# A gated attention and feed-forward kernel on one core: the first attention tile's transposes move into the last gate/up unit, and the last down groups are spread between the output products

## The chip, the cores and the metric

The kernel runs on one core of one Trainium2 chip. The metric is the device time of one execution in microseconds (us), as the median of several executions; lower is better.

## The reference

The input `x` has 2048 rows of 576 values. A gate per row mixes two branches:

```python
g = sigmoid((x * gate_w).sum(-1, keepdims=True))
a = attention(x, wq, wk, wv, wo, beta)      # 32 heads of 18, 4 segments of 512 rows, with a memory carried on
b = (silu(x @ w_gate) * (x @ w_up)) @ w_down  # hidden width 4608
return g * a + (1 - g) * b
```

Inside the attention, each segment has softmax attention among its own 512 rows (`a_dot`) and a read of a memory of the earlier segments (`a_mem`); the two are mixed per head by `sigmoid(beta)`, and the result `o` is multiplied by `wo` (576 by 576). The four segments run one after another for the memory, which is empty for the first one.

## The kernel before

All matrix products are done in split form: a number is the sum of a high part (`hi`, made by ScalarE with a copy) and a low part (`lo`, made by VectorE as the source minus the high part), and a product becomes three matmuls, hi by hi, hi by lo and lo by hi.

The kernel first makes queries, keys, values and the memory reads and stores them in DRAM. The main part is a loop over 72 units: two halves of the rows (segments 2 and 3, then 0 and 1), and in each half 36 blocks of 128 hidden columns. In one unit, `seven(t, j)` issues seven blocks of seven matmuls, numbered j = 0 to 6, which give the gate and up products of that block for the half's 1024 rows (a seven-product scheme with sums of operands). ScalarE and VectorE turn the seven results into `silu(gate) * up`, in two row blocks, split into `hh` and `hl`. The order around a unit's end is: `seven(a, 4)`; ScalarE copies bank `a` to bank `xx` (line 1067); VectorE adds (1068); ScalarE loads the table for silu and does silu twice (1070, 1072), then loads the table for exp (989); `seven(y, 5)`; `seven(xx, 6)`, which adds to the bank that 1067 has filled; VectorE multiplies (1077, 1078); and the splits of the two row blocks to `hh` and `hl` follow (129 or 938 on ScalarE, 130 or 939 on VectorE). The banks a, xx and y are PSUM banks 0, 1 and 2.

Every third unit closes a group of three hidden blocks. The list `groups` then holds 16 down groups (8 row tiles by two column halves, of 320 and 256 columns). `down_group` issues nine matmuls for one of them (three hidden blocks by three split terms, line 856) into one PSUM bank and has VectorE add that bank to `ya` (line 861). In the middle of the kernel these groups are worked off in the next unit. The 16 groups of the very last unit have no next unit.

Work that must happen some steps later is put into `due` by `defer(k, fn)`; `beat()` takes out and runs one step's list. A unit has eight beats, k = 0 to 7, each after one of the `seven` blocks (two after block 5). Attention runs beside the units as a generator, one step per beat. When it has ended, `c_open` takes its memory over for the output stage: `wo` comes in six pieces of 96 columns (`wo_load`: a DMA, line 886; a high part on ScalarE, line 889; a low part on VectorE, line 890; three pieces for each column half of `wo`), and the first two attention tiles are loaded (`c_load`: `o`, line 895, and for rows with a memory `me`, line 899).

The output stage is the loop over n at the end, 16 tiles of 128 rows, written one tile ahead: step n prepares tile n and multiplies tile n - 1. `c_tr` prepares a tile: GpSimd adds `me` to `o` (911) and copies the last 64 columns (912), TensorE transposes five 128 by 128 blocks with the identity (915 to PSUM bank 5 or 6, 917 to bank 7), ScalarE and VectorE split the result into `oh` and `ol` (129, 130) and `os` (163, 164). `products` (line 152) multiplies a tile by one column half of `wo` in 14 matmuls into one of banks 0, 1, 2. VectorE then mixes with the feed-forward row tile `ff` (1127, 1128), and the rows are stored (1131, at the end 1133). `f_load` (906) fetches `ff` for the first half from DRAM. The down groups of the last unit are issued in the same loop, by `downs(k)`, and use banks 3 and 4 in turn.

The order on each engine is the order in which the Python code issues the instructions (`manual_schedule`); engines wait for one another through semaphores. All DMAs of this stage are issued from one queue, SP.

The tail that the change touches:

```python
ffs = {n: f_load(n) for n in range(2)}
for n in range(17):
    if n < 16:
        if n + 2 < 16:
            tiles[n + 2] = c_load(n + 2)
            ffs[n + 2] = f_load(n + 2)
        nxt = c_tr(*tiles.pop(n))
        downs(2 if n else 4)
    if n:
        ...
        for hf in range(2):
            t = chain_tile()
            products(t[:, :288], ops, w_mov(wos[hf], 288))
            downs(1)
            ...
    ops = nxt
```

Of the kernel before, what the change touches and what calls it, by code (L numbers as in the profile page):

```python
# [65 lines left out]
def gated_mix(ctx, tc, xT, xrest, wf, wfr, wfh, wd, wv, wo, beta, cmask, ident, bmask, out):  # L66
# [61 lines left out]
    def split(hi, lo, src):  # L128
        nc.scalar.activation(hi, src, AF.Copy)  # L129
        nc.vector.tensor_sub(lo, src, f32(hi))  # L130
# [31 lines left out]
    def xs_split(xs, raw):  # L162
        nc.scalar.activation(xs, raw, AF.Copy)
        nc.vector.tensor_sub(xs[64:128], raw[64:128], f32(xs[64:128]))
# [47 lines left out]
    def w_load(f, u):  # L212
        r = raw_tile().rearrange("p (k n) -> p k n", n=P)
        nc.sync.dma_start(r, wf[f][:, u, 0:4])
        return r
# [30 lines left out]
    def r_fetch(f):  # L246
        nc.sync.dma_start(f32(rhs[f % 2][:96]).rearrange("p j n -> p (j n)"), rc[f // 4, :, f % 4])
# [441 lines left out]
    with ExitStack() as st:  # L689
# [3 lines left out]
        def defer(k, fn):  # L693
            while len(due) < k:
                due.append([])
            due[k - 1].append(fn)
# [8 lines left out]
        def w_fetch(f):  # L705
            ops = wops[1, f] = [None] * 7

            def one(j):
                ops[j] = op_tile()
                nc.sync.dma_start(f32(ops[j]).rearrange("p a k n -> p (a k n)"), wc[f, j])  # L710

            return [(j + 2 if f else FIRST[j], lambda j=j: one(j)) for j in range(7)]
# [153 lines left out]
        wos, tiles = [], {}  # L866
# [42 lines left out]
        def c_tr(o, me):  # L909
            if me is not None:  # L910
                nc.gpsimd.tensor_add(o[:, 0:D], o[:, 0:D], me)
            nc.gpsimd.tensor_copy(o[:, 576:640], o[:, 512:576])
            ta = half_tile([P, 4, P])
            for k in range(4):
                nc.tensor.transpose(ta[:, k], o[:, P * k:P * k + P], idt)
            tb = lone_tile([P, P])
            nc.tensor.transpose(tb, o[:, 512:640], idt)
            oh = cps[0].tile([P, 4, P], F32R, name="oh")
            ol = cps[0].tile([P, 4, P], F32R, name="ol")
            os_ = cps[0].tile([P, P], F32R, name="os")  # L920
            split(oh, ol, ta)
            xs_split(os_, tb)
            r = []
            for k in range(4):
                r += [oh[:, k], ol[:, k], oh[:, k]]
            return r + [os_, os_]
# [30 lines left out]
        def feed(half, f):  # L957
            return [(f // CH, i, hf, hs, ds, yas[half], half) for i in range(8) for hf in range(2)]
# [32 lines left out]
        def seven(t, j, first=True):  # L991
# [6 lines left out]
                    n += 1  # L998
            nc.tensor.matmul(t, rem[:, RPOS[j]], XR[j], start=False, stop=True, skip_group_check=True)  # L999

        draw = {}
        for o, fn in start:
            defer(o - 7, fn)
        for pos, (half, f) in enumerate(seq):
            if f == 0:
                yas[half] = yp.tile([P, 8, D], F32, name="ya")
            q = f % CH
            nxt = seq[pos + 1] if pos + 1 < len(seq) else None
            if q == 0 and f:
                groups += feed(half, f - 1)  # L1010
            plan = []
            if nxt:
                plan += w_fetch(nxt[1]) if nxt[0] and nxt[1] < KEPT else w_make(*nxt)
                if nxt != (0, 1):
                    plan.append((1 if nxt[1] else 10, lambda f=nxt[1]: r_fetch(f)))
                for n, h in enumerate(BLOCKS.get(pos, ())):
                    plan += r_block(h, 4 * n)
                if f + 2 < FT:
                    wraw_of[f + 2] = [None, None]
                    for u in range(2):  # L1020
                        plan.append(((2, 5)[u] if f or not half else 5 + u, lambda u=u, f=f: wraw_of[f + 2].__setitem__(u, w_load(f + 2, u))))
            if pos == FT - 2:
                X2, XR2 = [[None, None] for _ in range(7)], [None] * 7
                plan += [(o + 8, fn) for o, fn in x_second(X2, XR2)]
            for o, fn in plan:
                defer(o + 1, fn)
            step = [0]

            def tick():
                k = step[0]  # L1030
                step[0] += 1
                if k == 0:
                    while stores:
                        nc.sync.dma_start(*stores.pop(0))
                if half == 0:
                    if (q, k) in ((0, 3), (1, 3), (2, 2)):
                        draw[f] = d_load(f)
                    if (q, k) in ((1, 1), (1, 7), (2, 4)):
                        g = f - 1 if k == 1 else f
                        ds[half, g] = d_split(g, draw.pop(g))  # L1040
                elif (q, k) in ((1, 0), (1, 2), (2, 1)):
                    g = f - 1 if k == 0 else f
                    ds[half, g] = d_fetch(g)
                beat(k, half)

            ops, rem = wops.pop((half, f)), rhs[f % 2]
            hh = fp.tile([P, 2, L], F32R, name="hh")
            hl = fp.tile([P, 2, L], F32R, name="hl")
            hs[half, f] = hh, hl
            a, y, xx = a_tile(), y_tile(), x_tile()  # L1050
            p5, sg0, sg1 = (row_tile() for _ in range(3))
            seven(a, 0)
            nc.scalar.activation(xx, a, AF.Copy)  # L1053
            tick()
            seven(y, 1)
            nc.scalar.activation(p5, y, AF.Copy)
            tick()
            seven(a, 2, False)
            y = y_tile()
            nc.vector.tensor_add(y, a, p5)  # L1060
            tick()
            seven(xx, 3, False)
            nc.scalar.activation(sg0, xx, AF.Copy)  # L1063
            tick()
            seven(a, 4, False)
            xx = x_tile()
            nc.scalar.activation(xx, a, AF.Copy)  # L1067
            nc.vector.tensor_add(p5, a, p5)  # L1068
            tick()
            nc.scalar.activation(sg0, sg0, AF.Silu)  # L1070
            seven(y, 5, False)
            nc.scalar.activation(sg1, y, AF.Silu)
            exp_table()
            tick()
            tick()
            seven(xx, 6, False)
            nc.vector.tensor_mul(sg0, xx, sg0)
            nc.vector.tensor_mul(sg1, p5, sg1)
            if q == CH - 1:
                defer(2, lambda t=(hh[:, 0], hl[:, 0], sg0): split(*t))  # L1080
            else:
                split_by(2, hh[:, 0], hl[:, 0], sg0)
            split_by(3, hh[:, 1], hl[:, 1], sg1)
            tick()
            assert not groups
            if f == FT - 1:
                groups += feed(half, f)
                if half == 0:
                    for n in range(BREAK):
                        beat(None if n > 1 else n)  # L1090
                    XO, XR = X2, XR2
                    assert not groups
# [13 lines left out]
        def downs(k):  # L1106
            for _ in range(min(k, len(groups))):
                down_group(*groups.pop(0))
# [4 lines that stand above are left out]
                if n + 2 < 16:  # L1113
                    tiles[n + 2] = c_load(n + 2)
                    ffs[n + 2] = f_load(n + 2)
                nxt = c_tr(*tiles.pop(n))
                downs(2 if n else 4)
            if n:
                tt = order[n - 1]
                ff = ffs.pop(n - 1)  # L1120
                for hf in range(2):
                    c = slice(288 * hf, 288 * hf + 288)
# [3 lines that stand above are left out]
                    if hf == 0:  # L1126
                        nc.vector.tensor_scalar_mul(ff, ff, g1[:, tt:tt + 1])
                    nc.vector.scalar_tensor_tensor(ff[:, c], t[:, :288], gg[:, tt:tt + 1], ff[:, c],
                                                   op0=OP.mult, op1=OP.add)
                    if hf == 0 and sent:  # L1130
                        nc.sync.dma_start(*sent.pop(0))
                    if n == 16:
                        nc.sync.dma_start(out[0, P * tt:P * tt + P, c], ff[:, c])
                if n < 16:
                    sent.append((out[0, P * tt:P * tt + P, :], ff))
            ops = nxt
# [54 lines left out]
```

## Time and profile before

| what | value |
|---|---|
| median of 3 runs | 1755.48 us (1752.46 to 1756.5) |
| the profiled execution's own time | 1755.81 us |
| its span, first to last instruction | 1754.1 us |
| granted TensorE clock, mean | 0.995 |
| TensorE (PE) busy | 1718.9 us, 98% |
| VectorE (DVE) busy | 1373.2 us, 78% |
| ScalarE (ACT) busy | 1094.7 us, 62% |
| GpSimd (POOL) busy | 935.5 us, 53% |

The execution's own time is 1.7 us longer than the span; what lies outside the span is launch and end. In a timeline row, the columns are the start (us from the span's start), the length, the engine, the line, the operation, what it writes and reads, the count, and in brackets the time that the engine stood idle just before and what released it. PEld is TensorE's loading of weights, which runs beside its matmuls. Matmuls overlap, so the pace of TensorE is the distance between starts and not the length of one.

### The profile page before, as it was taken

The page shows a single profiled execution, that of the slowest core. Times are in us where ns is not written, and L with a number is a line of the kernel's source. Part 1 is how long each engine was busy: PE and PEld are TensorE (multiplying, and loading weights), DVE is VectorE, ACT ScalarE, POOL GpSimd, SP SyncE. Part 2 cuts the span into 40 slices and gives each one's busy share as a digit, 9 for nine tenths or more (in the row PEclk, how much of TensorE's full clock was granted, in tenths as well). Part 3 has the DMA queues.
Part 4 walks back from the last instruction along what each step waited for, and adds up shares of the span by engine and source line. Part 5 has one row for each costly group of instructions (what it writes and reads, how often), then busy time and mean ns, then how long its engine had stood idle before and what let it go on. Part 6 is the DMA issues. An engine that isn't in the chain of part 4 may idle for free.

```text
span 1754.1 us, 34945 instructions
## 1 busy us (share of the span) xinstructions
PE 1718.9 (98%) x11868; PEld 1487.7 (85%) x11868; DVE 1373.2 (78%) x3239; ACT 1094.7 (62%) x2201; POOL 935.5 (53%) x1194
## 2 busy tenths in 40 slices
PE   9999999999999999999999999999999999999999
PEld 7898878888888878887887888888888888888799
DVE  6567577988898888898889777788788777887655
ACT  7665575765776577576666756665765576556511
POOL 4434546566665656665566455555555555555221
PEclk9999999999999999999999999999999999999999
DMA  8653589999998988998889976876787667866544
GB/s 288 220 188 113 168 285 188 214 203 191 231 217 189 199 193 194 178 219 189 192 175 248 282 170 141 187 169 160 160 179 170 148 165 179 169 127 156 167 132 140
DMA packets 524003, 328.06 MB, mean 187 GB/s; under 512 B 411184, under 2 KB 460336, under 8 KB 523824
## 3 DMA queue, kind: packets, MB, share of 16 engines
q1 hardware_dynamic: 523824, 325.83, 76.6%
q8 instruction: 93, 1.52, 0.4%
q14 instruction: 86, 0.70, 0.1%
HBM read 165.76 MB, written 76.09 MB: 138 GB/s over the span
## 4 chain that ended last, share of the span: by engine, by line
PE 77%; ACT 9%; DVE 5%; issue 3%; DMA 3%; POOL 2%; SPq 1%; DVEq 0%; ACTq 0%; POOLq 0%
PE bank L996 29%; PE bank L856 24%; PE bank L152 10%; PE bank L999 5%; PE bank L725 3%; PE bank L773 2%; ACT L1070 1%; PE bank L774 1%; DMA pt<-p 1%; ACT L989 1%; ACT pe L743 1%; PE bank L411 1%; DVE hl L939 1%; PE bank L457 1%; DMA draw<-in_wd_dram 1%
## 5 line engine op out<-in xcount | busy, mean ns | idle before, releaser
L758 POOL TENSOR_TENSOR p<-pe,p 128x512 f16<-128x512 f32 x320 | 374.3, 1170 | 459.2 <-DVE p L757 440.4
L856 PE MATMUL bank<-dw,hh 128*128 128x320 f32 (+1 forms) x2304 | 490.4, 306 | 4.3 <-ACT hh L129 2.1
L856 PEld LDWEIGHTS bank<-dw,hh 128*128 128x128 f32 x2304 | 382.8, 190 | 15.7 <-DVE ya L861 2.6
L743 ACT ACTIVATE pe<-bank,mb 128x512 f32<-128x512 f32 (+3 forms) x512 | 246.1, 522 | 219.9 <-DVE mb L731 217.0
L856 PE MATMUL bank<-dw,hl 128*128 128x320 f32 (+1 forms) x1152 | 341.2, 296 | 0.2 <-DVE hl L130 0.2
L731 DVE CUSTOM_DVE_ANT_0 scr<-bank,cm 128x512 bf16<-128x512 f32 (+3 forms) x512 | 246.1, 481 | 7.4 <-PE bank L725 0.6
L856 PEld LDWEIGHTS bank<-dw,hl 128*128 128x128 f32 x1152 | 218.7, 190 | 0.4 <-DVE hl L130 0.4
L861 DVE TENSOR_TENSOR ya<-bank,ya 128x320 f32<-128x320 f32 x352 | 157.5, 452 | 78.2 <-PE bank L856 77.3
L999 PE MATMUL bank<-xr,rh 128*128 128x512 f32 x504 | 197.0, 391 | 0.0
L751 POOL TENSOR_SCALAR_AFFINE_SELECT pe<-pe 128x256 f32<-128x256 f32 (+1 forms) x320 | 150.8, 472 | 31.2 <-ACT pe L743 25.0
L757 DVE CAST p<-pe 128x512 f16<-128x512 f32 x320 | 145.2, 454 | 2.9 <-DMA pt<-p 2.7
L257 POOL TENSOR_TENSOR ws<-raw 128x256 f32<-128x256 f32 x140 | 122.9, 878 | 19.6 <-DMA raw<-in_wf_dram 6.4
L725 PE MATMUL bank<-kst,qst 108*128 108x512 bf16 (+3 forms) x512 | 125.4, 306 | 5.2 <-ACT pe L743 5.1
L999 PEld LDWEIGHTS bank<-xr,rh 128*128 128x128 f32 x504 | 95.0, 188 | 20.5
L939 DVE TENSOR_TENSOR hl<-row,hh 128x512 fp32r<-128x512 f32 x120 | 100.9, 841 | 10.4 <-ACT hh L938 10.0
L1063 ACT ACTIVATE row<-bank 128x512 f32<-128x512 f32 x72 | 43.1, 598 | 96.2 <-PE bank L999 96.1
L1068 DVE TENSOR_TENSOR row<-bank,row 128x512 f32<-128x512 f32 x72 | 49.6, 689 | 56.5 <-ACT bank L1067 56.3
L1070 ACT ACT_TABLE_LOAD x72 | 92.4, 1283 | 1.3
L989 ACT ACT_TABLE_LOAD x72 | 92.4, 1283 | 1.0
L773 PE MATMUL bank<-v,pt 128*128 128x57 bf16 x1280 | 77.3, 188 | 8.5 <-DMA pt<-p 5.3
L1053 ACT ACTIVATE bank<-bank 128x512 f32<-128x512 f32 x72 | 41.7, 579 | 66.7 <-PE bank L999 66.7
L773 PEld LDWEIGHTS <-pt 128*128 128x128 f16 x1280 | 69.6, 96 | 16.1 <-issue 7.2
(2165 smaller groups left out, 4127.2 us busy)
## 6 DMA issues: line engine op xcount, KB each, us to landing
raw<-in_wf_dram SPq DMA_DIRECT2D x140, 256.0 KB
rh<-rc SPq DMA_DIRECT2D x72, 336.0 KB
dc<-dw SPq DMA_DIRECT2D x36, 576.0 KB
dw<-dc SPq DMA_DIRECT2D x36, 576.0 KB
stk<-q SPq DMA_DIRECT2D x32, 384.0 KB
draw<-in_wd_dram SPq DMA_DIRECT2D x36, 288.0 KB
rc<-rt SPq DMA_DIRECT2D x42, 224.0 KB
vd<-vps SPq DMA_DIRECT2D x8, 912.0 KB
```

Source lines behind the costliest of these rows:

```text
L152: nc.tensor.matmul(t, st[n], mv[n], start=(n == 0), stop=(n == 13))
L725: nc.tensor.matmul(t[:, c:c + w], qs[:KR, pr, P * i:P * i + P], ks[:KR, pr, 0:w], start=True, stop=True)
L731: nc.vector.tensor_tensor_reduce(scr[:, :w], t[:, c:c + w], cm[:, L - w:L], -SCALE, 3.0e38, OP.add, OP.min, m[:, k:k + 1])
L743: nc.scalar.activation(pe[:, c:c + w], t[:, c:c + w], AF.Exp, bias=m[:, k:k + 1], scale=SCALE)
L751: nc.gpsimd.affine_select(d, d, pattern=pat, compare_op=OP.is_ge, fill=0.0, base=0, channel_multiplier=1)
L757: nc.vector.tensor_copy(p[:, 0], pe)
L758: nc.gpsimd.tensor_sub(p[:, 1], pe, p[:, 0])
L773: nc.tensor.matmul(t[:, pr, i, :], pt[:, c], v, start=(n == 0), stop=False, skip_group_check=True)
L856: nc.tensor.matmul(t, p, q[:, cs], start=(n == 0), stop=(n == 3 * CH - 1))
L861: nc.vector.tensor_add(ya[:, i, cs], t, ya[:, i, cs])
L996: nc.tensor.matmul(t, w[:, p, z], x[z][:, q], start=first and n == 0, stop=False, skip_group_check=True)
L999: nc.tensor.matmul(t, rem[:, RPOS[j]], XR[j], start=False, stop=True, skip_group_check=True)
```

## The change

The last unit (the only one without a next unit) gets one more planned step: three steps on in its plan, which is at its beat k = 3, right after `seven(xx, 3)`, `c_tr` of tile 0 is issued. The loop at the end then takes the result from the list `early` at n = 0. The numbers of down groups per step change as well: none at n = 0 and none ahead of the products at n = 1. Before, the 16 groups lay 4, 4, 4, 4 on n = 0, 1, 2, 3; now they lie 2, 4, 4, 4, 2 on n = 1 to 5. No instruction is added or removed.

```diff
+        early = []
         draw = {}
         ...
             plan = []
+            if not nxt:
+                plan.append((3, lambda: early.append(c_tr(*tiles.pop(0)))))
             if nxt:
         ...
                     tiles[n + 2] = c_load(n + 2)
                     ffs[n + 2] = f_load(n + 2)
-                nxt = c_tr(*tiles.pop(n))
-                downs(2 if n else 4)
+                nxt = c_tr(*tiles.pop(n)) if n else early.pop()
+                downs(2 if n > 1 else 0)
```

The order of TensorE's work from the last unit's block 3 on, where tr(n) is the five transposes of tile n, P(n, h) the 14 products of tile n with column half h, and g0, g1, ... the down groups:

```text
before: seven 3, seven 4, seven 5, seven 6, tr0, g0, g1, g2, g3, tr1, g4, g5, P(0,0), g6, P(0,1), g7, tr2, ...
after:  seven 3, tr0, seven 4, seven 5, seven 6, tr1, P(0,0), g0, P(0,1), g1, tr2, g2, g3, P(1,0), g4, P(1,1), g5, tr3, ...
```

On ScalarE the two splits of tile 0 (129, 163) now stand behind the fourth `wo` piece (889) and ahead of the copy 1067 of the last unit. On VectorE the two splits of tile 0 (130, 164) now stand ahead of 1068, with the `wo` pieces three and four (890), 1077 and 1078 behind them. GpSimd's order and SP's order of DMAs are the same as before.

## The prediction

> **What bounds the kernel now.** I read the page's engine shares first, then busy time by stretches around the last unit, then the waits of TensorE in that stretch, then each engine's timeline there.
>
> ```profile
> span 1754.1 us, 34945 instructions
> PE 1718.9 (98%) x11868; PEld 1487.7 (85%) x11868; DVE 1373.2 (78%) x3239; ACT 1094.7 (62%) x2201; POOL 935.5 (53%) x1194
> ```
>
> The stretches after the last unit (length, then busy time of PE, PEld, DVE, ACT, POOL, granted clock, DMA share, GB/s):
>
> ```profile
> 1659.00:1662.50 3.50, 1.38 (x11) 1.11 (x9) 2.94 (x6) 3.47 (x7) 0.55 (x1) 1.00 1.10 360
> 1662.50:1668.00 5.50, 4.18 (x27) 3.72 (x28) 4.07 (x8) 1.13 (x3) 3.51 (x4) 1.00 0.62 231
> 1668.00:1695.50 27.50, 27.50 (x212) 27.50 (x211) 12.28 (x26) 2.30 (x6) 5.57 (x6) 1.00 0.37 119
> ```
>
> The waits of TensorE from 1653 to 1669:
>
> ```profile
> PE bank L856 <- ACT hh L129: 2.1, 1, 2.1
> PE bank L856 <- DVE ya L861: 1.1, 1, 1.1
> ```
>
> TensorE is busy 98% of the span, so an edit can only win where it stands still or by taking work off it, and this one takes none off. The stretches show where it stands still: 1.38 of 3.50 us busy right after the last unit, 4.18 of 5.50 us next, and then 27.50 of 27.50. The waits name what ends it: the first down group waits for the high part `hh` of the last hidden block, and the third for VectorE to empty its bank. TensorE's timeline gives the places.
>
> ```profile
> 1653.58 1.52 PE L996 MATMUL bank<-xo,wo__22970 128*128 128x512 f32 x6
> 1655.17 1.52 PE L996 MATMUL bank<-xo,wo__22994 128*128 128x512 f32 x6
> 1657.07 1.65 PE L996 MATMUL bank<-xo,wo__23009 128*128 128x512 f32 x6 [0.15 <-ACT bank L1067]
> 1658.79 0.60 PE L915 MATMUL bank<-idt,o 128*128 128x128 f32 x4
> 1659.26 0.54 PE L856 MATMUL bank<-dw,hh 128*128 128x320 f32 x2
> ...
> 1662.52 0.56 PE L856 MATMUL bank<-dw,hh 128*128 128x320 f32 x2 [2.14 <-ACT hh L129]
> 1663.49 0.40 PE L856 MATMUL bank<-dw,hh 128*128 128x256 f32 x2
> 1665.86 0.56 PE L856 MATMUL bank<-dw,hh 128*128 128x320 f32 x2 [1.14 <-DVE ya L861]
> 1668.83 0.54 PE L856 MATMUL bank<-dw,hh 128*128 128x320 f32 x2
> ```
>
> The chain of waits further on:
>
> ```profile
> 1671.47 1.86 PE bank L152 x14
> 1673.33 1.32 PE bank L856 x9
> ...
> 1676.51 1.08 PE bank L856 x9
> ```
>
> In the timeline, the first three rows start blocks 4, 5 and 6 of the last unit; block 5 follows block 4 by 1.59 us, so block 6 could start at 1656.76 and starts at 1657.07: 0.31 us late. Then tr0 at 1658.79 (0.47 us to the next start), g0 at 1659.26, g1 at 1663.49, g2 at 1665.86, and after g3 and tr1 comes g4 at 1668.83. The rows of the chain give the pace without waits: a product half 1.86 us, a down group 1.32 us (320 columns) or 1.08 us (256).
>
> From 1658.79 to 1668.83 are 10.04 us. The work in it is tr0 0.47, four groups 2 x 1.32 + 2 x 1.08 = 4.80, and tr1 0.47: 5.74 us. So 4.30 us are lost here, and the 0.31 us before block 6. That is all that the change can win: at most 4.6 us, 0.26% of the time. What a measurement of this kernel can tell from no change is about 0.2%, 3.5 us.
>
> **The change, part by part.** I follow each engine through the changed order. The timelines of ScalarE, VectorE and GpSimd have the rows that set the times:
>
> ```profile
> 1655.93 0.61 ACT L889 ACTIVATE wo<-raw 128x480 fp32r<-128x480 f32 x1 [0.98 <-DMA raw<-in_wo_dram]
> 1656.44 0.58 ACT L1067 ACTIVATE bank<-bank 128x512 f32<-128x512 f32 x1
> 1660.87 1.08 ACT L889 ACTIVATE wo<-raw 128x480 fp32r<-128x480 f32 x2
> 1661.85 0.61 ACT L129 ACTIVATE hh<-row 128x512 fp32r<-128x512 f32 x1
> 1662.89 0.57 ACT L129 ACTIVATE oh<-bank 128x512 fp32r<-128x512 f32 x1
> 1663.37 0.26 ACT L163 ACTIVATE os<-bank 128x128 fp32r<-128x128 f32 x1
> ...
> 1657.05 0.69 DVE L1068 TENSOR_TENSOR row<-bank,row 128x512 f32<-128x512 f32 x1 [2.27 <-ACT bank L1067]
> 1657.66 2.42 DVE L890 TENSOR_TENSOR wo<-raw,wo 128x480 fp32r<-128x480 f32 x2
> 1662.50 0.69 DVE L130 TENSOR_TENSOR hl<-row,hh 128x512 fp32r<-128x512 f32 x1 [0.35 <-ACT hh L129]
> 1663.11 0.65 DVE L890 TENSOR_TENSOR wo<-raw,wo 128x480 fp32r<-128x480 f32 x1
> 1663.67 0.68 DVE L939 TENSOR_TENSOR hl<-row,hh 128x512 fp32r<-128x512 f32 x1
> 1664.28 0.68 DVE L130 TENSOR_TENSOR ol<-bank,oh 128x512 fp32r<-128x512 f32 x1
> 1664.99 0.29 DVE L164 TENSOR_TENSOR os<-bank,os 64x128 fp32r<-64x128 f32 x1
> ...
> 1650.34 0.31 POOL L912 COPY o<-o 128x64 f32<-128x64 f32 x1
> 1657.51 1.44 POOL L911 TENSOR_TENSOR o<-o,me 128x576 f32<-128x576 f32 x1 [6.86 <-DMA me<-med]
> 1659.01 0.55 POOL L912 COPY o<-o 128x64 f32<-128x64 f32 x1
> 1664.01 1.62 POOL L911 TENSOR_TENSOR o<-o,me 128x576 f32<-128x576 f32 x1 [4.44 <-DMA me<-med]
> ```
>
> Transposes moved (tr0). GpSimd has tile 0 ready at 1650.65 (the 912 row), TensorE comes to it after block 3 at 1653.58: no wait, 0.47 us. Blocks 4 and 5 start at 1654.05 and 1655.64, and block 6 could start at 1657.23.
>
> ScalarE's two splits moved. They are queued behind the fourth `wo` piece (889), which waited for its DMA until 1655.93, and the copy 1067, on which block 6 waits, is now queued behind them. By the rows' starts, 889 to the next is 0.51 us, the `oh` split to the next 0.48, and the `os` split 0.26: `oh` starts at 1656.44, `os` at 1656.92, 1067 at 1657.18 instead of 1656.44. So 0.74 us go on the path: block 6 starts at 1657.81 instead of 1657.07 and ends its pace at 1659.53. All that ScalarE does after 1067 follows back to back up to `hh` (table, two silus, table, two `wo` pieces), so `hh` is 0.74 us later too: it starts at 1662.59, and the row of 1662.52 for TensorE becomes 1663.26. The next two steps hide part of it.
>
> tr1 and products. tr1 needs GpSimd's tile 1, done at 1659.56 (1659.01 + 0.55), so it runs to 1660.03. P(0,0) runs to 1661.89. Its low parts: VectorE's order is now `ol` and `os` of tile 0 (0.61 + 0.3 us, from 1657.05), 1068 to 1658.6, and then the `wo` pieces three and four; GpSimd's add ends at 1658.95, so piece three is done at 1659.6, before the third matmul of P(0,0) at 1660.3. No wait.
>
> g0. Two of its three blocks run from 1661.89 to 1662.77, then it waits for `hh` at 1663.26. Before, g0 ended at 1663.49, with `hh` and the wait for `hl` in it; the same 0.74 us later is 1664.23. So the wait of 2.1 us shrinks to 0.5.
>
> P(0,1). It needs the last `wo` piece's low part, 0.74 us later than 1663.76: 1664.50. Its third matmul comes at 1664.49. It just fits, and it ends at 1666.09; g1 to 1667.17. tr2 needs GpSimd's tile 2: the add is ready to start at 1664.01 and lasts 1.44 us, and after the copy the tile is there by about 1666.4. No wait; tr2 to 1667.64.
>
> g2's bank. VectorE must have emptied g0's bank, behind the second `hl` (939), `ol` and `os` of tile 1. I estimate from the rows that 939 is held up by GpSimd's add until 1665.93, as the two 890 were at 1657.66 (2.42 us for two that take 0.65 each, with an add of 1.44 us beside them). Then 0.6 for 939, 1.0 for the splits, 0.5 for the bank: 1668.0. So g2 waits 0.36 us instead of the 1.14 before.
>
> Sum. The changed kernel starts g2 at 1668.0 with tr0, tr1, tr2, P(0,0), P(0,1), g0 and g1 done. The kernel before starts g4 at 1668.83 with tr0, tr1 and g0 to g3 done. The changed one is ahead by tr2 0.47 and two halves 3.72, less g2 and g3 2.40: 1.79 us of work. The gain is 1668.83 - 1668.0 + 1.79 = 2.6 us.
>
> After that. Two groups move from n = 0 to n = 4 and 5, where TensorE has no gaps to fill, at 1.32 + 1.08 us, already in the sum. The tail is bound by TensorE (27.50 of 27.50 us). SP's order and GpSimd's are unchanged; the tile loads wait for the buffers of transposed tiles, which come free earlier. I put later effects at nothing; what would uncover them is a load landing after its tile's turn.
>
> The profiled execution took 1755.81 us; less 2.6 is 1753.2. The median of the runs is 0.33 us lower, so it goes to 1752.9. I forecast 1753.0.
>
> [...] The 890 row is VectorE work with both inputs in SBUF, which took 2.42 us instead of 1.3 while GpSimd added. In the row of 1664.01 it is the other way round: GpSimd's add took 1.62 us, where 939 had started before it. [...]
>
> **The rivals.**
>
> First, the early landing: ScalarE's fourth piece does not hold up the copy, since its DMA lands 0.7 us or more earlier. Then `hh` is ready at 1662.5 as before, g0 ends at 1663.3, P(0,1) waits 0.2 us for the last low part and ends at 1665.4, g2 starts at 1666.9 with its bank free: 1668.83 - 1666.9 + 1.79 = 3.7 us, 1752.1. For it: landing times hang on a queue at a DMA share of 1.10 and vary. Against it: in this trace the piece ended a ScalarE wait of 0.98 us.
>
> Second, the lost lock: the last `wo` piece's low part on VectorE should start at 1663.85, GpSimd's add at 1664.01. If the add is first by 0.2 us, the piece waits to 1665.45 and is ready at 1666.1; P(0,1) stands from 1664.49 to 1666.1, ends at 1667.7, and g2 starts at 1669.25: 1.4 us gained, 1754.4. For it: only 0.16 us decide. Against it: nothing else on VectorE is queued ahead.
>
> Third, slower: the `wo` pieces become the wait. Before, P(0,0) came at about 1671.3 and the last low part at 1663.76, 7.5 us of slack; now P(0,1) needs it at 1664.49 and has none. Each microsecond that the last two pieces land late is then one of TensorE, past the point where ScalarE is free for them (1660.87). From 2.6 us late on the kernel is slower than before; 6.1 us late costs 0.2%, at 1759.3. For it: the DMA engines are full in that stretch. Against it: 889 ran the two at 1660.87 without a wait for a DMA, and SP's order is unchanged.
>
> That the change does not do what it says is excluded by the order of instructions: the five transposes do stand after block 3.
>
> **How the numbers follow.** Forecast 0.42, early landing 0.30, lost lock 0.18, late pieces 0.10. The three runs before lie 4 us apart, so a median of a few can be off by 1.5 us. The forecast's 2.6 us then read as over 3.5 about one time in three (0.15), the early landing's 3.7 six in ten (0.18), the lost lock's seldom (0.03): faster 0.36. Slower by over 0.2% needs the late pieces (0.08). The rest, 0.56, is within 0.2%. The range reaches from the early landing less 1.9 us (1750.2) to the lost lock with 1.6 us of scatter (1756.0).
>
> **What would show it.** Right: tr0 in the unit at no wait; 1067 about 0.7 us later; `products` ahead of g0; the wait for `hh` at about 0.5 us instead of 2.1; no wait above 0.5 us for `ya`; and the rest of the tail without a gap. Wrong: a wait of TensorE at the transposes (tile 0 late), at P(0,1) for the last `wo` piece of over 1 us, or at later transposes for GpSimd; or a time beyond the range with this stretch as forecast, which would put the cause elsewhere.

## The result: 4.8 us faster

| | kernel before | changed kernel |
|---|---|---|
| median of 22 runs | 1755.44 us | 1750.65 us |
| lowest to highest | 1749.49 to 1761.92 us | 1746.59 to 1753.4 us |
| profiled execution, its span | 1755.81 us, 1754.1 us | 1749.81 us, 1748.1 us |

The ratio is 0.9974 with a 95% interval of 0.9967 to 0.9982: between 3.2 and 5.8 us faster. The page of the changed kernel has the same shares as before:

```profile
span 1748.1 us, 34944 instructions
PE 1716.3 (98%) x11868; PEld 1484.9 (85%) x11868; DVE 1372.0 (78%) x3239; ACT 1094.5 (63%) x2201; POOL 935.1 (53%) x1194
```

TensorE's timeline after the last unit's block 3:

```profile
1650.89 0.60 PE L915 MATMUL bank<-idt,o 128*128 128x128 f32 x4
...
1651.35 1.64 PE L996 MATMUL bank<-xo,wo__22970 128*128 128x512 f32 x6
...
1654.72 1.65 PE L996 MATMUL bank<-xo,wo__23009 128*128 128x512 f32 x6
...
1656.44 0.60 PE L915 MATMUL bank<-idt,o 128*128 128x128 f32 x4
...
1656.91 0.38 PE L152 MATMUL bank<-wo,oh 128*128 128x288 f32 x1
...
1658.84 0.46 PE L856 MATMUL bank<-dw,hh 128*128 128x320 f32 x2
...
1660.17 0.55 PE L856 MATMUL bank<-dw,hh 128*128 128x320 f32 x2 [0.29 <-ACT hh L129]
1660.89 0.41 PE L856 MATMUL bank<-dw,hl 128*128 128x320 f32 x1 [0.17 <-DVE hl L130]
1661.15 0.30 PE L152 MATMUL bank<-wo,oh 128*128 128x288 f32 x1
...
1663.15 0.40 PE L856 MATMUL bank<-dw,hh 128*128 128x256 f32 x2
...
1664.24 0.60 PE L915 MATMUL bank<-idt,o 128*128 128x128 f32 x4
...
1664.70 0.54 PE L856 MATMUL bank<-dw,hh 128*128 128x320 f32 x2
```

The rows are, in order: tr0, blocks 4 and 6, tr1, the start of P(0,0), g0, its two short waits, P(0,1), g1, tr2, and g2. The waits of 2.14 us for `hh` and 1.14 us for g0's bank have become 0.29 us and nothing.

To compare kernels that reach this place a few us apart, I use one length from here on. The **tail** is the time from the start of TensorE's next work after block 3 to the end of the span. It was 1754.1 - 1653.58 = 100.5 us before and is 1748.1 - 1650.89 = 97.2 us now: 3.3 us less. The other 2.7 us between the two spans lie ahead of anything the change touches.

### The profile page after: what moved, and what is told of

It reads as the page before. It is cut to its first block, busy times and chain, and to the rows that moved or that the text cites. A ratio compares the mean times of both kernels' runs of the same rounds, so it can differ in the third digit from the quotient of the medians.

```text
span 1748.1 us, 34944 instructions
## 1 busy us (share of the span) xinstructions
PE 1716.3 (98%) x11868; PEld 1484.9 (85%) x11868; DVE 1372.0 (78%) x3239; ACT 1094.5 (63%) x2201; POOL 935.1 (53%) x1194
## 4 chain that ended last, share of the span: by engine, by line
PE 76%; ACT 9%; DVE 5%; issue 4%; DMA 3%; POOL 3%; SPq 0%; DVEq 0%; ACTq 0%; POOLq 0%
PE bank L996 29%; PE bank L856 23%; PE bank L152 9%; PE bank L999 5%; PE bank L725 3%; PE bank L773 2%; ACT L1073 1%; DMA pt<-p 1%; PE bank L774 1%; ACT L989 1%; PE bank L411 1%; ACT pe L743 1%; DVE scr L731 1%; PE bank L457 1%; POOL ws L257 1%
## 5 line engine op out<-in xcount | busy, mean ns | idle before, releaser
L939 DVE TENSOR_TENSOR hl<-row,hh 128x512 fp32r<-128x512 f32 x120 | 101.7, 847 | 10.7 <-ACT hh L938 10.3
L152 PE MATMUL bank<-xo,qhi 128*128 128x512 f32 x264 | 83.1, 396 | 0.0
```

Source lines behind the costliest of these rows:

```text
L152: nc.tensor.matmul(t, st[n], mv[n], start=(n == 0), stop=(n == 13))
```

## The experiments

**The same two programs again.** Is the part ahead of the tail shorter too, or is that scatter?

> The changed kernel once more, beside a second run of the kernel before. I call tail the time from the end of block 3's matmuls in the last unit to the end of the span: 100.5 us in the profile before, 97.2 us in the profile after, so 3.3 us of the 6.0 us between the two spans. Theory A (the gain is TensorE's standstill after the last unit, filled with products): the tail is 97.2 us again, within 0.5, and the rest of the difference between two spans lies ahead of it and changes its sign or size. Theory B (the change also shortens what lies ahead of the last unit, for example through where memory lies): the tail differs by 3.3 us and the part ahead is shorter by 1 to 3 us again.

> The kernel before, unchanged. Theory A: the tail is 100.5 us within 0.7 us (its waits hang on when the fourth wo piece lands), and the part ahead of it scatters by a few us from run to run. Theory B: the part ahead is again 1 to 3 us longer than that of the changed kernel in the same call.

The changed kernel came to 1750.39 us (ratio 0.9975, 0.9965 to 0.9985), with a tail of 1747.7 - 1650.40 = 97.3 us. The kernel before came to 1756.11 us against its own other runs on that chip (ratio 1.0012, 1.0002 to 1.0021, for the same program, so a difference of some 0.1% is not to be trusted in such a comparison). Its block 3 ended at 1649.98 us, earlier than in the changed kernel (1650.89, 1650.40): theory B falls, the part ahead only scatters. The granted clock, the share of full speed at which the profile shows TensorE running, goes with that scatter. Ahead of block 3's end TensorE's clock stood at half for some 10 us in this profile and in both of the changed kernel, and for some 17 us in the first profile before. Over all thirteen profiles of this document, with tr0 taken off where it stands ahead, block 3 ends at 1649.9 to 1650.9 us where that time was 10 us (once at 1652.5), at 1651.7 to 1652.8 where it was 14, and at 1653.6 where it was 17. But the tail of the second profile before was 1752.6 - 1649.98 = 102.6 us, 2.1 us more than in the first profile, and outside theory A's 0.7 us. TensorE's timeline there:

```profile
1658.62 0.56 PE L856 MATMUL bank<-dw,hh 128*128 128x320 f32 x2 [2.12 <-ACT hh L129]
...
1661.96 0.90 PE L856 MATMUL bank<-dw,hh 128*128 128x320 f32 x2 [0.94 <-DVE ya L861]
...
1662.93 0.74 PE L856 MATMUL bank<-dw,hh 128*128 128x320 f32 x2
```

The waits are as before, yet the matmuls after them are slow: a pair of 320 columns is 0.74 us long instead of 0.46. The busy time by stretches of this run has the reason (columns as before: length, busy time of PE, PEld, DVE, ACT and POOL, granted clock, DMA share, GB/s):

```profile
1655.00:1660.00 5.00, 2.71 (x19) 2.19 (x18) 4.44 (x8) 4.70 (x10) 0.61 (x2) 1.00 1.10 363
1660.00:1665.00 5.00, 4.06 (x19) 3.77 (x19) 2.41 (x6) 0.00 (x0) 3.56 (x4) 0.55 0.40 149
1665.00:1670.00 5.00, 5.00 (x33) 5.00 (x33) 2.17 (x5) 0.77 (x2) 0.00 (x0) 0.77 0.27 75
```

The granted clock, third column from the end, is 0.55 and 0.77. In finer stretches it fell to 0.50 at about 1660.5, 2 us after the standstill, and came back at about 1667.3 us. In the first profile before it was 1.00 throughout this stretch, and in the changed kernel's profile too:

```profile
1660.00:1665.00 5.00, 4.66 (x33) 4.28 (x34) 4.75 (x10) 1.35 (x5) 3.35 (x3) 1.00 1.05 390
1665.00:1670.00 5.00, 5.00 (x39) 5.00 (x38) 2.19 (x5) 0.70 (x2) 2.11 (x4) 1.00 0.69 233
```

**One half of the change: transposes early, groups as before.**

```diff
-                downs(2 if n > 1 else 0)
+                downs(2 if n else 4)
```

> Half of the change: tile 0 is transposed in the last unit, but the down groups stay at 4, 4, 4, 4 on n = 0 to 3. Theory A (products must fill the wait for hh): the wait of g0 for hh stays at 2 us or more, since the transposes no longer stand ahead of it; only the wait for g0's bank shrinks, by up to 1.1 us, since tile 0's two VectorE splits have gone from the queue ahead of it. The tail is 99.5 to 100.5 us. Rival (the moved transposes are the gain): the tail is 97 to 98 us.

1755.03 us, ratio 1.0001 (0.9992 to 1.0010). TensorE's only wait in the stretch:

```profile
PE bank L856 <- ACT hh L129: 2.7, 1, 2.7
```

The wait for `hh` grew, the wait for the bank is gone, both as theory A has it. The tail is 1753.5 - 1651.69 = 101.8 us: above the forecast of 99.5 to 100.5, with a clock that fell here too (0.53 from 1660 to 1665), and 0.8 us below the kernel before with a fallen clock. The moved transposes alone are not the gain.

**The other half: groups spread, transposes as before** (`downs(2 if n > 1 else 0)` in the kernel before).

> The other half: tile 0 is transposed at n = 0 as before, and the down groups lie 2, 4, 4, 4, 2 on n = 1 to 5. Theory A: the products of tile 0 come first, but need tile 0's low part, which VectorE makes only after both hl splits (1664.3 to 1665.0 in the trace before), so TensorE waits about 5 us at the first products; the tail is about 101.4 us, 0.9 us longer than before. Rival (the order of groups is the gain, wherever tile 0 is transposed): the tail is 97 to 98.5 us.

1757.53 us, ratio 1.0018 (1.0009 to 1.0027). That is slower, as theory A has it, if by little beside the 1.0012 that the unchanged kernel showed in the same comparison. The wait is another than the one I named:

```profile
PE bank L917 <- DVE os L164: 5.3, 1, 5.3
```

TensorE stands at tr1's fifth transpose. That block always goes to PSUM bank 7, and tile 0's `os` split, late in VectorE's queue, had not emptied it. The tail is 1756.1 - 1652.49 = 103.6 us, with the clock fallen, 1.0 us more than in the second profile before. Each half alone gives nothing or less; the gain needs both.

**ScalarE's queue ahead of `hh`.** First the two moved splits:

```diff
-                plan.append((3, lambda: early.append(c_tr(*tiles.pop(0)))))
+                plan.append((2, lambda: early.append(c_tr(*tiles.pop(0)))))
```

> The changed kernel with tile 0 transposed one beat earlier, after block 2: ScalarE's two splits of tile 0 then stand ahead of the fourth wo piece instead of behind it. My theory that these two splits lie on the path (they moved the copy ahead of block 6, and with it hh, by 0.3 us in the profile after): the copy comes right after the fourth piece again, block 6 is late by 0.1 us or less beyond before, and the wait for hh in g0 goes to nothing; the tail is 96.7 to 97.0 us, 0.2 to 0.5 us less than after. Rival (they lie beside the path): the tail stays at 97.2 us. Second rival: tile 0 is not ready on GpSimd that early, and TensorE waits at the transposes.

1749.78 us, ratio 0.9979 (0.9969 to 0.9989). Block 6 followed block 5 without delay (1653.49 after 1651.90), and the wait for `hh` was 0.18 us. The tail, with the 0.47 us of tr0 that now lie ahead of it added, is 97.0 us against 97.2 and 97.3 in the two profiles of the changed kernel: the splits cost the path some 0.2 us by these, which no median resolves.

Then the table of exp, which nothing needs any more when attention has ended (the same edit in both kernels):

```diff
-            exp_table()
+            if pos < len(seq) - 2:
+                exp_table()
             tick()
```

> The kernel before, without the load of the exp table in the last two units, where no exp is left to do (attention has ended); the silu table then stays loaded, so ScalarE's queue in the last unit is shorter by two loads of 1.28 us and one small instruction. Theory A (the wait for hh is the end of ScalarE's back-to-back queue from the copy on): hh comes about 2.7 us earlier, until VectorE's multiply (1660.7 in the trace before) or the wo pieces' landing ends it, so about 1.5 to 2.5 us earlier; the wait of 2.1 us in g0 falls below 0.7 us and the tail is 97.5 to 99 us. Rival (hh waits for VectorE or a DMA, not for ScalarE's queue): the tail stays above 100 us.

> The changed kernel without the exp table in the last two units. Theory A: the changed kernel has only 0.5 us of waits for hh and hl left, so the two together win little more: the tail is 96.4 to 96.9 us against 97.2 us, far less than the sum of both gains. Rival (the two gains are independent): the tail is 95 to 96 us.

> Both additions to the changed kernel: transposes after block 2, and no exp table in the last two units. Theory A: no wait is left for ScalarE; what is left is the pace of the matmuls, and the tail is 96.2 to 96.8 us, at or just below the kernel without the exp table. Rival: the wo pieces' landing now sets the products of the second column half, and the tail stays at 97 us.

In the kernel before it did nothing: 1755.17 us, ratio 1.0001 (0.9991 to 1.0010), tail 1751.1 - 1650.81 = 100.3 us with a wait of 2.3 us for `hh`. Theory A fails here, and ScalarE's timeline shows why:

```profile
1657.39 0.60 ACT L889 ACTIVATE wo<-raw 128x480 fp32r<-128x480 f32 x1 [2.61 <-DMA raw<-in_wo_dram]
1658.31 0.60 ACT L889 ACTIVATE wo<-raw 128x480 fp32r<-128x480 f32 x1 [0.32 <-DMA raw<-in_wo_dram]
1658.82 0.61 ACT L129 ACTIVATE hh<-row 128x512 fp32r<-128x512 f32 x1
```

Two loads of tables of 1.28 us each are gone from the queue, and the time won turned into a wait for the last two `wo` pieces, which stand ahead of `hh` in the queue. The two limits had lain close together: `hh` starts 8.01 us after block 3's end, where it was 8.27 before. The clock fell in this profile too, to 0.50 from 1659.4 to 1662.8, but cost nothing here: VectorE emptied g0's bank only at 1662.78, and g2, which needs it, started at 1662.84. In the changed kernel the edit gave 1749.79 us (0.9975, 0.9966 to 0.9985) with a tail of 1749.7 - 1653.60 = 96.1 us, 0.3 below the forecast, and no wait of TensorE at all there; with the transposes one beat earlier as well, 1750.74 us (0.9970, 0.9959 to 0.9980), where the pieces landed later and g0 waited 0.87 us for `hh` (tail 97.7 us with tr0 added, above what either theory had). Which of them is fastest can't be told from the medians.

**`hh` ahead of the last two `wo` pieces**, with the exp table left out as above:

```diff
+            lag = 3 if n > 7 else 0
-            defer(n + 5, lambda: nc.scalar.activation(wos...
-            defer(n + 7, lambda: nc.vector.tensor_sub(wos...
+            defer(n + 5 + lag, lambda: nc.scalar.activation(wos...
+            defer(n + 7 + lag, lambda: nc.vector.tensor_sub(wos...
```

> The kernel before without the exp table in the last two units, and with the splits of the last two wo pieces three beats later, so that hh stands ahead of them in ScalarE's queue. The run without the table alone did not shorten the wait for hh (2.3 us), since ScalarE then waited for the landing of those pieces (2.6 us). Theory E (hh was late for two reasons of about the same length, the table loads and the wo pieces queued ahead of it): with both gone, hh waits only for VectorE's multiply, g0 waits 0.5 to 1.2 us, TensorE has no standstill above 1.3 us, the clock stays at 1.00, and the tail is 99 to 100.3 us. Rival (hh is late because of VectorE's multiply): g0 waits 2 us again and the tail is above 100.3 us.

> The changed kernel with the same two edits: no exp table in the last two units, hh ahead of the last two wo pieces. Theory E: nothing is left to wait for in the stretch; the tail is 96.0 to 96.5 us, as in the changed kernel without the table (96.1), and the landing of the wo pieces no longer shows in g0. It should be the fastest of all: ratio to the kernel before 0.9966 to 0.9974. Rival (the last wo pieces, now later, hold up the products of the second column half): a wait of 0.5 us or more at P(0,1), tail 96.6 to 97.5 us.

In the kernel before: 1753.79 us, ratio 0.9996 (0.9985 to 1.0006). TensorE:

```profile
1659.72 0.56 PE L856 MATMUL bank<-dw,hh 128*128 128x320 f32 x2 [1.00 <-ACT hh L129]
...
1664.05 0.90 PE L856 MATMUL bank<-dw,hh 128*128 128x320 f32 x2 [2.12 <-DVE ya L861]
```

The third pair of g0, which needs `hh`, came 1.4 us earlier than in the first profile before, counted from block 3's end, and waited 1.00 us, as theory E has it. But VectorE came to g0's bank only 0.4 us earlier, so that wait grew from 1.14 to 2.12 us, and the clock fell at its end. The tail is 1753.8 - 1652.15 = 101.7 us, where theory E had at most 100.3: the standstill only moved. In the changed kernel: 1750.70 us, ratio 0.9982 (0.9972 to 0.9993), tail 1748.3 - 1650.85 = 97.5 us, with one wait, at a place neither theory had:

```profile
1657.46 0.66 PE L916 MATMUL bank<-idt,o 128*128 128x128 f32 x4 [1.10 <-POOL o L912]
```

tr1 waits for tile 1, whose load landed late in this run: GpSimd's add, which waited for it, starts 5.00 us after block 3's end, and 3.61 us after it in the first profile of the changed kernel. Theory E had this run as the fastest of all (0.9966 to 0.9974); it is not faster than the change as it stands.

**The clock by itself.** Does the standstill bring the low clock?

```diff
                 nxt = c_tr(*tiles.pop(n))
+                if n == 0:
+                    t = y_tile()
+                    for k in range(14):
+                        nc.tensor.matmul(t[:, :320], hs[1, FT - 3][0][:, 0, 0:P], ds[1, FT - 3][:, 0, 0:320],
+                                         start=(k == 0), stop=(k == 13))
```

> The kernel before with 14 extra matmuls (320 columns, result not used) between tr0 and g0, 2.06 us by their pace, so that TensorE is busy where it waited for hh. They add work and take none away, and hh and hl come when they did. The runs so far: four of five profiles of kernels with the standstill show the granted clock at 0.50 for some 6 us after it, no profile of a kernel with the products there does. Theory C (the standstill itself brings the low clock, and that is the part of the gain that the refill does not explain): the clock stays at 1.00 from 1640 to 1700, the tail is 100.3 to 101.0 us (100.5 in the profile before, which had no low clock, 102.6 in the second one, which had), and the median is 1 to 2 us below that of the kernel before (ratio 0.9988 to 0.9994), though there is more work. Theory D (the low clock comes from elsewhere and only happened to be missing in the changed kernel): the clock falls as before, the tail is 102 to 103 us and the ratio is 1.000.

```profile
1655.00:1660.00 5.00, 5.00 (x27) 3.91 (x26) 3.95 (x5) 4.94 (x8) 2.47 (x2) 1.00 1.09 345
1660.00:1665.00 5.00, 3.69 (x25) 3.14 (x24) 4.39 (x9) 2.63 (x6) 1.72 (x2) 1.00 1.02 377
1665.00:1670.00 5.00, 5.00 (x39) 5.00 (x40) 2.37 (x6) 0.77 (x2) 1.68 (x2) 1.00 0.20 45
```

With the extra matmuls in the gap the clock stayed at 1.00, and the tail is 1753.1 - 1652.76 = 100.3 us, in theory C's range and 2.3 us below the second profile before. The median did not show it: 1754.63 us, ratio 0.9998 (0.9988 to 1.0009). Theory C had 0.9988 to 0.9994, theory D 1.000, and the interval holds both. The mean granted clock of the 12 executions is 0.9959, against 0.9950 in the 29 of the kernel before beside them; but it is 0.9958 in the ten of the kernel with `hh` ahead of the pieces, whose profile shows the drop. One profile for theory C, a median and a mean clock that can't tell: the cause is likely and not settled.

What many runs have is their mean granted clock. Over 89 executions of the kernel before it is 0.9952, over 73 of the changed kernel and its variants 0.9962. Among those 89, an execution with a clock higher by 0.001 is 1.1 us shorter (slope of a line through them). So I estimate that the changed kernel's higher clock is worth about 1.1 us of the median, on top of the tail's 3.3 us at full clock. Together 4.4 us, against 4.8 measured (3.2 to 5.8). A mean over the whole run does not say where in it the clock was low, so the 1.1 us are not shown to come from this stretch.

The rest of the runs bears the other part out. The executions with a mean clock of 0.995, 0.996 and 0.997 took 1754.5, 1753.6 and 1753.1 us on average among those 89, and 1751.3, 1751.2 and 1749.3 us among the 31 of the changed kernel itself. At the same clock the change is thus worth 3.2, 2.4 and 3.8 us, about what the tail shows.

## Why the prediction was right, and where it was short

The direction, the refilled standstill and the range held (1750.65 in 1750.2 to 1756.0), but the likeliest case, a gain of 2.6 us that reads as no change, was too small: 4.8 us were measured. That the result lies inside the range, 0.45 us from its end, is in part luck: that end was the early landing's 3.7 us with 1.9 us of scatter, and what by the estimate above brought the time there beyond the tail's 3.3 us, a better clock, was in no term. There is a slip in it as well: the forecast is counted from the median of the runs, the rivals from the profiled execution, which is 0.33 us longer. Counted alike, the early landing is at 1751.8, not 1752.1. By its own steps:

Transposes moved: right. tr0 ran without a wait, in 0.46 us (1650.89 to 1651.35).

ScalarE's two splits: right in kind, but I had put them too large. ScalarE's timeline after:

```profile
1652.92 0.60 ACT L889 ACTIVATE wo<-raw 128x480 fp32r<-128x480 f32 x1 [0.75 <-DMA raw<-in_wo_dram]
1653.43 0.58 ACT L129 ACTIVATE oh<-bank 128x512 fp32r<-128x512 f32 x1
1653.90 0.27 ACT L163 ACTIVATE os<-bank 128x128 fp32r<-128x128 f32 x1
1654.06 0.60 ACT L1070 ACTIVATE bank<-bank 128x512 f32<-128x512 f32 x1
...
1659.50 0.62 ACT L129 ACTIVATE hh<-row 128x512 fp32r<-128x512 f32 x1
```

The copy (now line 1070) comes 3.17 us after block 3's end instead of 2.86 (1656.44 - 1653.58): 0.31 us later, where I had 0.74. The fourth piece landed 0.32 us earlier, and the `os` split takes 0.16 us of the queue, not 0.26. That is part of the way to the first rival, the early landing, which needs 0.7 us.

g0: right. The wait for `hh` is 0.29 us, where I had 0.5, and the one for `hl` 0.17, as before.

g2's bank: wrong. I held VectorE's second `hl` (939) up behind GpSimd's add. VectorE's timeline after:

```profile
1660.76 0.65 DVE L890 TENSOR_TENSOR wo<-raw,wo 128x480 fp32r<-128x480 f32 x1
1661.33 0.69 DVE L939 TENSOR_TENSOR hl<-row,hh 128x512 fp32r<-128x512 f32 x1
...
1662.97 0.49 DVE L861 TENSOR_TENSOR ya<-bank,ya 128x320 f32<-128x320 f32 x1
```

GpSimd's:

```profile
1654.50 1.43 POOL L911 TENSOR_TENSOR o<-o,me 128x576 f32<-128x576 f32 x1 [6.62 <-DMA me<-med]
...
1661.47 1.83 POOL L911 TENSOR_TENSOR o<-o,me 128x576 f32<-128x576 f32 x1 [4.93 <-DMA me<-med]
```

939 had started 0.14 us before the add, ran at its own length of 0.69 us, and the add took 1.83 us instead of 1.43. This goes back to the splits: they held VectorE's last `wo` piece and 939 up by 0.34 us where I had 0.74, and the add came 0.15 us later than before. The bank was empty at 1663.5, and g2 followed tr2 without a wait. I had the order wrong. Where 939 started first elsewhere, 0.08 us ahead of the add in the run with the transposes early alone, 0.27 us in the second profile before and 0.28 us in the second of the changed kernel, it took 0.68 or 0.69 us and the add 1.88, 1.68 and 1.71 us. Where the add started first, 0.15 us ahead of the two 890 in the first profile before, it took 1.44 us and they 2.42 us, where one by itself takes 0.65. The second rival, in which the add starts ahead of the last `wo` piece, did not happen: the piece started 0.71 us before the add (1660.76, 1661.47).

In all, g2 starts 13.81 us after block 3's end (1664.70 - 1650.89), where the forecast had 14.42 (1668.0 - 1653.58). The 0.6 us make the gain of 2.6 into 3.2, and the tails of the two profiles differ by 3.3. The third rival, late `wo` pieces, did not show: P(0,1) took 2.00 us (1661.15 to 1663.15), P(0,0) 1.93 (1656.91 to 1658.84).

The step that failed is the ceiling: "that is all that the change can win". I read it from one profile, in which the granted clock was 1.00 throughout the stretch, and took the matmuls' pace after the standstill for given. Of six profiles with a standstill of 2 us or more here (the kernel before twice, and its four variants other than the one with extra matmuls), five show the clock at half for 3 to 7 us, from within the standstill, from its end or from up to 2 us after it; in the six profiles of the changed kernel and its variants it stayed at full speed there. Against the second profile before, the changed kernel's tail is 5.4 us shorter (102.6 against 97.2), more than the ceiling of 4.6. By the mean clocks that part is worth about 1.1 us of the median, an estimate; it was in no term and no rival. The median's interval, 3.2 to 5.8 us, would by itself leave the ceiling standing.

## What to carry to other kernels

Do not count a standstill of TensorE at its length alone: look at the granted clock of the stretch behind it, in more than one profile, since the same wait of 2.1 us had a clock of 1.00 behind it and a tail of 100.5 us in one, and a clock of 0.50 for 6.8 us and a tail of 102.6 us in the next. To fill a wait for a late operand, two things have to be moved together, work that does not need the operand and that work's own preparation; either alone gave nothing or a loss here (ratios 1.0001 and 1.0018, against 0.9974 for both). When two kernels are compared whose mean clock scatters from one execution to the next, compare executions with the same mean clock. And when a queue ends in a late result, shortening it helps only as far as the next limit: here the table loads, the landing of the `wo` pieces, VectorE's queue and the tile load lay within a microsecond or two of one another (with the table loads of 2 x 1.28 us gone, `hh` started 0.26 us earlier; with g0's third pair 1.4 us earlier, VectorE came to its bank 0.4 us earlier).

## What the runs showed of the hardware

The granted clock fell to 0.50 at standstills of TensorE of 2.1 to 5.3 us, but not each time: the wait of 2.1 us was followed by it in one of two profiles of the same program. In two profiles it fell within 0.1 us of the standstill's end, in one 1.9 us after it, and in the two halves of the change while TensorE still stood. It then stayed low for 3.4 us (without the exp table, 1659.4 to 1662.8, and with `hh` ahead of the pieces) or for twice that (6.8 us, in the second profile before from 1660.5 to 1667.3, and in both halves of the change). No run here shows what sets these lengths, or why the same wait of 2.1 us was followed by the fall in one profile and not in the other.
